# A windowed-attention and mixer kernel: batch 2's q and k turned over by DMA instead of TensorE

## The chip, the cores and the metric

The kernel runs on one core of a Trainium2 chip. The metric is the device time of one execution in microseconds (us): for the kernel before, the median of 3 runs is 300.8 us (300.75, 302.64 and 300.8). One further execution was profiled; the views below are of that one.

## What is computed

Eight batches of attention with 8 heads over 576 positions of 64 elements. Heads 0 to 3 see a plain window of the last 32 positions, heads 4 to 7 a dilated one (every fourth of the last 128). The result, with the heads side by side as 512 channels, goes through a mixer: two matrices over the positions, added back, and two over the channels, added back.

```
q, k, v: [8, 8, 576, 64] float32
scores = (q @ k^T) / 8
plain heads:   0 <= i-j < 32                    dilated heads: 0 <= i-j < 128 and (i-j) % 4 == 0
attn   = softmax over the allowed j;  x = attn @ v   -> [8, 576, 512]
h = relu(x^T @ w_tok1) @ w_tok2;      u = x + h^T      (w_tok1 576x256, w_tok2 256x576)
out = u + relu(u @ w_ch1) @ w_ch2                      (w_ch1 512x1536, w_ch2 1536x512)
```

## The kernel before, in words

**Stages of a batch.** q, k and v are loaded in float32 by DMAs issued on SyncE's queue (SP; `emit_loads_qk`, `load_steps`, `load_v`), cast to float16 by GpSimd (POOL; `cast_steps`, L272), and q and k are turned over so that the 64 elements of two heads lie on the partitions. The four pairs of heads are called hp 0 to 3: hp 0 and 1 are plain, hp 2 and 3 dilated. The turned q stands in `qz[hp]`, one plane for each head with the other head's half zero, k in `kt[hp]`. `scores_plain` (L402) and `scores_dil` (L432) make the scores of one hp in three parts: part 0 and part 1 are the main blocks of the first and the second head, part 2 the rest of both. ScalarE (ACT) takes the exponential into `attp[hp]` or `attd[hp-2]`. From batch 2 on, GpSimd then multiplies the two heads' blocks by the band of allowed pairs (L428, L429 for plain, L454, L455 for dilated); batches 0 and 1 have the band added on TensorE (PE) instead. `values` (L458) makes attention times v for one head, VectorE (DVE) divides by the sums into `xn`, `emit_h1` and `emit_u` are the mixer over positions, `emit_uT` (L530) turns its result over, and `gen_main` (L590) is the mixer over channels: 24 groups `gp` of four matmuls, then the groups `yp`, whose sums DVE adds and SP stores.

**Two ways of turning q and k over.** `transposes` (L291) does it on TensorE: four transposes of 128x128 for q and one for the last 64 positions of q and k, four for k, for each hp; then copies out of PSUM on DVE and ACT. The other way is taken by `by_dma(b)` (L330), before for b >= 3. `dma_steps` (L333) issues five DMA transposes on SP: the tails (`tta`), then q and k of hp 0 and 1 (`qta`, `kra`), then q and k of hp 2 and 3. `place_steps` (L348) copies from there: `plain(hp)` is three copies on GpSimd for hp 0 or 1 (L358 for `kt`, L360 for the two planes of `qz`); `tails`, `dil(0)`, `dil(1)` and `dil_k` are DVE copies (L354, L355, L364, L369). The dilated scores then read k straight from `kra`.

**The order of work.** Nothing is scheduled by a planner at run time. The start (batch 0, L672 to L831) is written out by hand. Then iteration b runs `gen_main(b)`, and `interleave` (L648) puts the stages of the next batches between its groups: each step has a due time in us from the iteration's start, each group and step a cost that is added to a running clock, and a step is emitted once the clock has reached its due time. So the due times give one order of emission, and each engine, and each DMA queue, works through its own share of that order strictly from front to back. A step whose due time comes after the last group of the iteration is emitted at its end, in order of due times.

Iteration 0 holds batch 1's scores, values and mixer over positions, the loads and casts of batch 2, and, before the change, the transposes and scores of batch 2's hp 0 and 1. Iteration 1 holds hp 2 and 3 of batch 2, then its values and mixer, and then the DMA way for batch 3. In the order before, SP meets at the end of iteration 0: the load of v of batch 2 (eight DMAs, L205, due 24.0), the two stores of `yp` s = 2, the two of s = 3, then batch 3's q and k. GpSimd meets the nine casts of q and k of batch 2, the multiplication of hp 0's scores, the eight casts of v, with the multiplication of hp 1 between them.

Of the kernel before, what the change touches and what calls it, by code (L numbers as in the profile page):

```python
# [69 lines left out]
def kernel(  # L70
# [108 lines left out]
    def new_qk(b):  # L179
        for nm in ("q", "k"):  # L180
            for i in range(2):
                l32[(b, nm, i)] = sb.tile([128, 4, 4, D], FP32, tag=f"l_{nm}{i}", bufs=1,
                                          name=f"l_{nm}_{b}_{i}")
        l32[(b, "t")] = sb.tile([128, H, D], FP32, tag="lt", bufs=1, name=f"lt_{b}")

    def load_qk(b, nm, h0, h1, eng):
        i = h0 // 4
        eng.dma_start(
            out=l32[(b, nm, i)][:, h0 - 4 * i:h1 - 4 * i].rearrange("m h r d -> m h (r d)"),
            in_=SRC[nm][b, h0:h1, 0:512, :].rearrange("h (m r) d -> m h (r d)", r=4))  # L190

    def load_tail(b, nm, eng):
        r0 = 64 * (nm == "k")
        eng.dma_start(out=l32[(b, "t")][r0:r0 + 64],
                      in_=SRC[nm][b, :, 512:S, :].rearrange("h s d -> s h d"))
# [20 lines left out]
    def load_v(b):  # L216
        for step in load_v_steps(b):
            step()
# [19 lines left out]
    def emit_loads_qk(b):  # L238
        new_qk(b)
        for nm in ("q", "k"):  # L240
            load_tail(b, nm, nc.sync)
        for h0 in (0, 4):
            for nm in ("q", "k"):
                load_qk(b, nm, h0, h0 + 4, nc.sync)
# [43 lines left out]
    def natural(ap):  # L288
        return ap.rearrange("p (m r) -> p m r", r=4)
# [38 lines left out]
            copy(eng, natural(kt[hp][:, 512:S]), grid[:, :, MR:RS].rearrange("p r m -> p m r"))  # L328

    def by_dma(b):  # L330
        return b >= 3

    def dma_steps(b):  # L333

        def turn_over(t, c):
            nc.sync.dma_start_transpose(out=t, in_=c)

        def half(t, nm, i):
            turn_over(t[:, 2 * i:2 * i + 2].rearrange("p a r m -> p (a r) m"),
                      c16[(b, nm)][:, 2 * i:2 * i + 2].rearrange("m a r h d -> m (a r h d)"))  # L340

        steps = [lambda: turn_over(tta, c16[(b, "t")].rearrange("m h d -> m (h d)"))]
        for i in range(2):
            for t, nm in ((qta, "q"), (kra, "k")):
                steps.append(lambda t=t, nm=nm, i=i: half(t, nm, i))
        return steps

    def place_steps(b):  # L348

        halves = [slice(0, 64), slice(64, 128)]  # L350

        def tails():
            for h in range(2):
                nc.vector.tensor_copy(out=qza[halves[h], :, h, 512:S], in_=tta[halves[h], :, 0:64])  # L354
            nc.vector.tensor_copy(out=kta[:, :, 512:S], in_=tta[:, :, 64:128])  # L355

        def plain(hp):
            nc.gpsimd.tensor_copy(out=natural(kt[hp][:, 0:512]), in_=kra[:, hp].rearrange("p r m -> p m r"))  # L358
            for h in range(2):
                nc.gpsimd.tensor_copy(out=natural(qz[hp][halves[h], h, 0:512]),  # L360
                                      in_=qta[halves[h], hp].rearrange("p r m -> p m r"))

        def dil(h):
            nc.vector.tensor_copy(out=qza[halves[h], 2:4, h, 0:512],  # L364
                                  in_=qta[halves[h], 2:4].rearrange("p a r m -> p a (r m)"))

        def dil_k():
            for hp in (2, 3):
                nc.vector.tensor_copy(out=natural(kt[hp][:, 384:512]),  # L369
                                      in_=kra[:, hp, :, 96:128].rearrange("p r m -> p m r"))  # L370

        return ([lambda hp=hp: plain(hp) for hp in range(2)],
                [tails] + [lambda h=h: dil(h) for h in range(2)] + [dil_k])
# [180 lines left out]
    def score_steps(b, t0, dt, offs=(0.0, 0.7, 2.0), places=None):  # L554

        steps = []
        for hp in range(4):
            at, at_s = places[hp] if places else (t0 + hp * dt, t0 + hp * dt + dt)
            for nm in ("q", "k") if not by_dma(b) else ():
                steps.append((at + 0.9 * (nm == "k"), 0.28, lambda nm=nm, hp=hp: transposes(b, nm, hp)))  # L560
            g = (scores_plain if hp < 2 else scores_dil)(b, hp)
            for i in range(3):
                steps.append((at_s + offs[i], 0.21, lambda g=g: next(g)))
        return steps

    def value_steps(b, t0, dt):
        steps = []
        for h in range(H):
            def step(h=h):
                if h == 0:  # L570
                    xn[b] = sb.tile([128, 5, DM], FP16, tag="xn", bufs=2, name=f"xn_{b}")
                values(b, h)
            steps.append((t0 + dt * h, 0.29 if h < 4 else 0.18, step))
        return steps

    def mix_steps(b, t_h1, t_h1b, t_u, t_uT, du=1.0):
        if b % 2 == 0 and b // 2 not in u16t:
            u16t[b // 2] = sb.tile([128, DM], FP16, tag="u16t", bufs=2, name=f"u16t_{b // 2}")
        h1 = [sb.tile([128, DM], FP16, tag="h1", bufs=4, name=f"h1_{b}_{jb}") for jb in range(2)]
        steps = []  # L580
        for half, at in ((0, t_h1), (1, t_h1b)):
            for jb in range(2):
                steps.append((at + 0.9 * jb, 0.55, lambda jb=jb, half=half: emit_h1(b, jb, half, h1[jb])))
        for i, s in enumerate((4, 0, 1, 2, 3)):
            steps.append((t_u + du * i, 0.44, lambda s=s: emit_u(b, s, h1)))
        for i, cb in enumerate(CBS):
            steps.append((t_uT + 0.9 * i, 0.28, lambda cb=cb: emit_uT(b, cb)))
        return steps
# [136 lines left out]
    va = [st[2] for st in value_steps(0, 0.0, 1.0)]  # L725
# [107 lines left out]
    def at(t0, dt, fs):  # L833
        return [(t0 + dt * i, 0.0, f) for i, f in enumerate(fs)]

    for b in range(B):
        steps = []
        if b == 0:
            steps += score_steps(1, 0, 0, (0.0, 0.6, 1.3),
                                 ((14.0, 16.2), (15.4, 18.2), (17.6, 20.0), (19.0, 21.6)))  # L840
            steps += at(20.0, 0.35, casts1[9:])
            steps += at(20.0, 0.0, [lambda nm=nm: load_qk(2, nm, 4, 8, nc.sync) for nm in ("q", "k")])
            steps += at(24.0, 0.0, [lambda: load_v(2)])
            casts = cast_steps(2)
            va = value_steps(1, 21.7, 0.7)
            steps += va[:4] + [(p + 0.2, c, f) for p, c, f in va[4:]]
            steps += mix_steps(1, 25.6, 28.4, 30.4, 36.2, 1.1)
            steps += score_steps(2, 0, 0, (0.0, 0.7, 1.6),
                                 ((28.8, 31.4), (31.2, 34.6), (0, 0), (0, 0)))[:10]
            steps += at(24.5, 0.5, casts[:9]) + at(34.5, 0.3, casts[9:])  # L850
            steps += at(36.0, 0.0, [lambda: emit_loads_qk(3)])
        elif b == 1:
            late = score_steps(2, -4.3, 2.4, (0.0, 0.7, 1.6))
            va = value_steps(2, 4.2, 1.0)
            steps += late[10:] + va[:4] + [(9.6 + (0.0, 0.8, 2.8, 3.6)[i], c, f) for i, (_, c, f) in enumerate(va[4:])]
            steps += mix_steps(2, 10.8, 14.6, 17.2, 22.2)
            steps += score_steps(3, 22.2, 2.8) + at(9.0, 0.6, cast_steps(3))
            steps += at(6.0, 0.0, [lambda: load_v(3)]) + at(20.0, 0.9, load_steps(4))
            steps += at(15.0, 0.7, dma_steps(3)) + at(20.6, 0.4, place_steps(3)[0])
            steps += [(t, 0.0, f) for t, f in zip((21.6, 27.0, 27.8, 28.6), place_steps(3)[1])]  # L860
        else:
            if b + 1 < B:
                steps += value_steps(b + 1, 0.6, 1.1) + mix_steps(b + 1, 6.6, 10.6, 13.2, 18.2)
            if b + 2 < B:
                steps += at(2.0, 0.6, cast_steps(b + 2)) + score_steps(b + 2, 18.6, 2.7)
                steps += at(8.5, 0.7, dma_steps(b + 2)) + at(14.8, 0.4, place_steps(b + 2)[0])
                steps += [(t, 0.0, f) for t, f in zip((17.3, 21.8, 22.6, 23.4), place_steps(b + 2)[1])]
            if b + 3 < B:
                steps += at(13.0, 0.9, load_steps(b + 3))
        interleave(gen_main(b), steps)  # L870
# [30 lines left out]
```

## Time and profile before

| what | value |
|---|---|
| median of 3 runs | 300.8 us |
| the profiled execution, its own time | 300.74 us |
| its span from first to last instruction | 298.7 us |
| granted TensorE clock, mean | 0.997 |
| busy: PE, DVE, ACT, POOL | 286.8, 159.3, 140.8, 180.1 us |
| iteration 0, from the first `gp` to the next iteration's first | 29.8 to 69.8 us |
| iteration 1 | 69.8 to 107.1 us |

How to read the views: PE is TensorE's matmul, PEld its weight load, which overlaps. A row of the timeline gives the start in us from the span's beginning, the time that the group took, the engine, the line of the kernel, the operation, output and input with their shapes, and how many instructions are merged. What stands in brackets is the idle time of the engine before the group and what ended it. The time of a matmul is its whole passage; back to back, the next one starts earlier, so the cost of a group on a busy PE is the distance from its start to the next group's start. SPq rows are DMA issues on SyncE's queue: their time is that of the issue, and the landing stands in a column of its own on the page.

### The profile page before, as it was taken

What the parts mean: (1) busy time and instruction counts of PE and PEld (TensorE: products, weight loads), DVE (VectorE), ACT (ScalarE), POOL (GpSimd) and SP (SyncE); (2) the same over time, 40 slices, a digit from 0 to 9 for tenths busy, and PEclk for the clock granted to TensorE, in tenths of its full rate; (3) what the DMA queues carried; (4) which work ended last, traced back from release to release, by engine and by line L of the source; (5) the groups of instructions that cost most, each with busy time, mean ns of one, the idle gap of its engine ahead of it and who ended that gap; (6) DMA issues with size and microseconds to landing.
All of it is one profiled execution on the core that took longest, in us unless ns stands there. A gap on an engine that the chain in (4) does not pass through costs nothing.

```text
span 298.7 us, 7805 instructions
## 1 busy us (share of the span) xinstructions
PE 286.8 (96%) x3112; PEld 257.2 (86%) x3112; DVE 159.3 (53%) x357; ACT 140.8 (47%) x319; POOL 180.1 (60%) x244
## 2 busy tenths in 40 slices
PE   5789999998999999999999999999999999999995
PEld 2687999987987999899987999899988999899794
DVE  5875438756737965643645254644745264532122
ACT  2853436377652545455545536365554535304500
POOL 7882056429998899739992999449992930000000
PEclk9999999999999999999999999999999999999998
DMA  7999999966997999984599749964551220022023
GB/s 219 270 212 177 214 312 222 326 165 188 286 196 128 279 288 154 280 211 151 69 205 276 211 111 153 307 139 146 120 55 35 72 72 0 3 71 72 2 70 105
DMA packets 91443, 49.10 MB, mean 164 GB/s; under 512 B 59760, under 2 KB 90352, under 8 KB 91408
## 3 DMA queue, kind: packets, MB, share of 16 engines
q1 hardware_dynamic: 87168, 43.53, 59.7%
q0 software_dynamic: 2640, 3.91, 7.4%
q10 hardware_dynamic: 1600, 1.18, 1.3%
q8 instruction: 24, 0.39, 0.6%
q14 instruction: 11, 0.09, 0.1%
HBM read 37.04 MB, written 9.44 MB: 156 GB/s over the span
## 4 chain that ended last, share of the span: by engine, by line
PE 92%; DVE 3%; DMA 2%; ACT 1%; issue 1%; ACTq 0%; POOLq 0%
PE gp L602 31%; PE yp L619 28%; PE sc L393 4%; PE h1p L499 4%; PE up L511 4%; PE yp L639 3%; DMA const<-consts 2%; PE sm L393 1%; PE tpu L548 1%; PE av L469 1%; PE h1p L497 1%; PE av L480 1%; PE tpu L540 1%; PE up L524 1%; PE av L467 1%; PE sc L391 1%
## 5 line engine op out<-in xcount | busy, mean ns | idle before, releaser
L602 PE MATMUL gp<-uT,w 128*128 128x288 f16 x768 | 109.9, 286 | 0.7 <-ACT uT L101 0.6
L619 PE MATMUL yp<-w,gt 128*128 128x256 f16 x756 | 95.6, 273 | 0.0
L107 ACT ACTIVATE gt<-gp 128x288 f16<-128x288 f32 x138 | 56.6, 410 | 72.1 <-PE gp L602 65.9
L602 PEld LDWEIGHTS <-w 128*128 128x128 f16 x768 | 83.1, 113 | 8.2 <-issue 1.2
L619 PEld LDWEIGHTS <-gt 128*128 128x128 f16 x768 | 75.9, 106 | 3.7
L113 POOL TENSOR_TENSOR attp<-attp,const 128x1280 f16<-128x1280 f16 (+1 forms) x24 | 36.0, 1529 | 32.9 <-ACT attp L422 32.9
L629 DVE TENSOR_TENSOR o<-yp,u 128x512 f32<-128x512 f32 x31 | 21.3, 689 | 50.6 <-PE yp L619 44.2
L109 DVE TENSOR_SCALAR gt<-gp 128x288 f16<-128x288 f32 x54 | 24.6, 455 | 35.5 <-PE gp L602 33.5
L113 POOL TENSOR_TENSOR attd<-attd,const 128x1024 f16<-128x1024 f16 (+1 forms) x24 | 32.8, 1397 | 0.0
L113 DVE TENSOR_TENSOR xn<-av,rec 128x320 f16<-128x320 f32 x64 | 31.5, 491 | 2.2
L393 PEld LDWEIGHTS <-kt 128*128 128x128 f16 x272 | 22.5, 101 | 3.1 <-DVE kt L302 1.6
L103 POOL CAST c_q<-l_q 128x512 f16<-128x512 f32 x31 | 18.9, 613 | 6.4 <-DMA l_q<-in_q_dram 5.7
L413 ACT ACTIVATE attp<-sc 128x480 f16<-128x480 f32 x32 | 18.0, 572 | 9.5 <-PE sc L393 9.4
L518 DVE TENSOR_TENSOR u<-up,xn 128x512 f16<-128x512 f32 x26 | 17.9, 691 | 8.0 <-PE up L511 8.0
L360 POOL COPY qz<-qt 64x512 f16<-64x512 f16 x20 | 21.4, 1072 | 0.6
L442 ACT ACTIVATE attd<-sc 128x512 f16<-128x512 f32 x32 | 18.9, 597 | 5.3 <-PE sc L393 4.7
L488 DVE RECIPROCAL rec<-av 128x5 f32<-128x5 f32 x64 | 12.2, 191 | 14.3 <-PE av L475 7.2
L393 PE MATMUL sc<-qz,kt 128*128 128x160 f16 (+1 forms) x144 | 18.6, 228 | 1.3 <-DVE kt L302 1.3
L103 POOL CAST c_k<-l_k 128x512 f16<-128x512 f32 x29 | 18.0, 622 | 3.0 <-DMA l_k<-in_k_dram 1.3
L101 ACT COPY uT<-tpu 128x576 f16<-128x576 f16 x15 | 9.6, 640 | 16.3 <-PE tpu L549 16.3
L107 ACT ACTIVATE h<-h1p 128x256 f16<-128x256 f32 x28 | 10.7, 383 | 10.1 <-PE h1p L499 8.0
L639 PE MATMUL yp<-w,gt 128*128 128x512 f16 x48 | 12.0, 379 | 0.0
(131 smaller groups left out, 444.4 us busy)
## 6 DMA issues: line engine op xcount, KB each, us to landing
out_dram<-o SPq DMA_DIRECT2D x72, 128.0 KB, 2.5
l_q<-in_q_dram SPq DMA_DIRECT2D x15, 512.0 KB, 6.4
l_k<-in_k_dram SPq DMA_DIRECT2D x14, 512.0 KB, 7.4
l_vn<-in_v_dram SPq DMA_DIRECT2D x32, 128.0 KB, 6.7
l_vd<-in_v_dram SPq DMA_DIRECT2D x16, 256.0 KB, 3.9
w<-in_moe_w_ch_dram POOLq DMA_DIRECT2D x6, 512.0 KB, 7.6
lt<-in_q_dram SPq DMA_DIRECT2D x8, 128.0 KB, 4.4
l_vt<-in_v_dram SPq DMA_DIRECT2D x8, 128.0 KB, 4.3
```

Source lines behind the costliest of these rows:

```text
L103: eng.tensor_copy(out=out, in_=in_)
L107: nc.scalar.activation(out=out, in_=in_, func=AF.Relu)
L109: eng.tensor_scalar_max(out=out, in0=in_, scalar1=0.0)
L113: eng.tensor_tensor(out=out, in0=x, in1=y, op=ALU.mult)
L360: nc.gpsimd.tensor_copy(out=natural(qz[hp][halves[h], h, 0:512]), in_=qta[halves[h], hp].rearrange("p r m -> p m r"))
L393: nc.tensor.matmul(out=out, lhsT=lhsT, rhs=qz[hp][:, h, queries], start=hide is None, stop=True)
L413: nc.scalar.activation(out=blocks[:, h, 0:3, 0:BLK], in_=p[:, 0:3 * BLK].rearrange("p (b c) -> p b c", c=BLK), func=AF.Exp, scale=0.125)
L442: nc.scalar.activation(out=a[:, h, 0:DTL], in_=p, func=AF.Exp, scale=0.125)
L602: nc.tensor.matmul(out=p[:, 0:288], lhsT=w3[cb][:, 512 * (mb // 4) + mb % 4:512 * (mb // 4) + 512:4], rhs=uT[(b, cb)][:, 288 * sh:288 * sh ...
L619: nc.tensor.matmul(out=p[:, c], lhsT=gt[(b // 2, mb)][:, a0:m0 + 512:4] if half else gt[(b // 2, mb)][:, a0:a0 + 128], rhs=w4[mb][:, c], s ...
L629: nc.vector.tensor_tensor(out=o32, in0=p, in1=u16[(b, s)], op=ALU.add)
L639: nc.tensor.matmul(out=p, lhsT=gt[(b // 2, mb)][:, 512:640], rhs=w4[mb], start=(mb == 0), stop=(mb == NMB - 1))
```

## The change

`by_dma` holds from b = 2 on, so batch 2's transposes on TensorE and their copies are gone and its dilated scores read `kra`. In iteration 0, instead of the transposes and the scores of hp 0 and 1, there are the five DMA transposes of batch 2 on SP, the six plain copies on GpSimd and, as the last step, the three tail copies on DVE. In iteration 1 all four hp's scores are due from 0.3 on, `dil(0)`, `dil(1)` and `dil_k` on DVE from 1.0 on, and the values and the mixer of batch 2 have later due times.

```
     def by_dma(b):
-        return b >= 3
+        return b >= 2
...
             steps += mix_steps(1, 25.6, 28.4, 30.4, 36.2, 1.1)
-            steps += score_steps(2, 0, 0, (0.0, 0.7, 1.6),
-                                 ((28.8, 31.4), (31.2, 34.6), (0, 0), (0, 0)))[:10]
             steps += at(24.5, 0.5, casts[:9]) + at(34.5, 0.3, casts[9:])
+            steps += [(t, 0.0, f) for t, f in zip((27.0, 30.0, 30.7, 33.0, 33.7), dma_steps(2))]
+            steps += at(34.4, 0.0, place_steps(2)[0]) + at(39.0, 0.0, place_steps(2)[1][:1])
             steps += at(36.0, 0.0, [lambda: emit_loads_qk(3)])
         elif b == 1:
-            late = score_steps(2, -4.3, 2.4, (0.0, 0.7, 1.6))
-            va = value_steps(2, 4.2, 1.0)
-            steps += late[10:] + va[:4] + [(9.6 + (0.0, 0.8, 2.8, 3.6)[i], c, f) for i, (_, c, f) in enumerate(va[4:])]
-            steps += mix_steps(2, 10.8, 14.6, 17.2, 22.2)
+            steps += score_steps(2, 0, 0, (0.0, 0.7, 1.6), ((0, 0.3), (0, 2.3), (0, 4.3), (0, 6.3)))
+            steps += at(1.0, 0.9, place_steps(2)[1][1:])
+            va = value_steps(2, 0.0, 1.0)
+            steps += [((6.8, 7.6, 9.0, 9.8, 12.0, 12.8, 14.8, 15.6)[i], c, f) for i, (_, c, f) in enumerate(va)]
+            steps += mix_steps(2, 11.6, 17.0, 19.4, 24.6)
```

Worked through `interleave`, the order after the change is as follows. SP: load of v of batch 2, stores of s = 2, transposes of the tails and of q of hp 0 and 1, stores of s = 3, transposes of k of hp 0 and 1, of q and of k of hp 2 and 3, batch 3's q and k. GpSimd: casts of q and k of batch 2, `plain(0)`, `plain(1)`, the eight casts of v, then the multiplications of hp 0, 1, 2, 3, then batch 3's casts. TensorE in iteration 1: one `gp` group, part 0 of hp 0, one group, part 1, two groups, part 2, part 0 of hp 1, one group, part 1, one group, part 2, and so on; the values of head 0 come behind ten groups, those of head 2 behind thirteen, of head 4 behind seventeen, of head 6 behind twenty.

## The prediction, as put on record before the change was run

> **What bounds the kernel now.** I read the page first, then busy time by stretch, then the timeline of each engine's queue around the edit.
>
> ```profile
> PE 286.8 (96%) x3112; PEld 257.2 (86%) x3112; DVE 159.3 (53%) x357; ACT 140.8 (47%) x319; POOL 180.1 (60%) x244
> ```
> ```profile
> 29.80:69.80 40.00, 38.73 (x468) 35.80 (x467) 23.91 (x53) 20.61 (x47) 17.46 (x30) 1.00 0.92 239
> 69.80:107.10 37.30, 36.94 (x412) 32.96 (x409) 25.98 (x49) 20.17 (x47) 35.18 (x43) 1.00 0.96 228
> ```
>
> The columns of the second fence are the stretch, its length, the busy time of PE, PEld, DVE, ACT and POOL, the granted clock, the DMA share and GB/s. The first row is iteration 0, the second iteration 1. TensorE is the bound in both: 38.73 of 40.00 and 36.94 of 37.30 us. Work taken off it comes back as time, and a wait put onto it is paid in full, for there is hardly any idle time later that would take it up. The second thing to see is GpSimd: half idle in iteration 0, but 35.18 of 37.30 us in iteration 1. The change adds GpSimd work just at this border.
>
> **What is taken off TensorE.** The turning of one q and its tail:
>
> ```profile
> 60.75 0.39 PE L297 MATMUL tp_q<-const,c_q 128*128 128x128 f16 x4
> 60.97 0.22 PE L317 MATMUL tp_q<-const,c_t 128*128 128x128 f16 x1
> 61.03 0.27 PE L497 MATMUL h1p<-xn,w1t 128*128 128x256 f16 x1
> ...
> 70.57 0.90 PE L602 MATMUL gp<-uT,w 128*128 128x288 f16 x6 [0.36 <-ACT uT L101]
> ```
>
> From start to start a q costs 0.28 us (60.75 to 61.03), a k 0.22 (60.75 to 60.97, the same four transposes). That is 0.50 for each hp, **2.0 us** for four. Their copies on DVE and ACT go too, but those engines are two thirds busy at most, so I count nothing for them. The scores are only moved: six parts of hp 0 and 1, about 0.2 us each, leave iteration 0. So iteration 1's first group, which ends about 70.8 (0.24 behind the last start above), would end at 70.8 - 1.0 - 1.2 = 68.6. The next instruction on TensorE is part 0 of hp 0, and it needs what GpSimd has placed. With the scores gone, the short waits in the chain of batch 1's mixer (0.36 above) may grow by some tenths; that only shifts 68.6, and the wait that follows ends with GpSimd and not with TensorE.
>
> **When the placing can start.** SP's queue and the issues of the DMA transposes of batch 3, which show what those of batch 2 will cost:
>
> ```profile
> 54.84 4.21 SPq L205 DMA_DIRECT2D l_vn<-in_v_dram  x4
> ...
> 62.06 0.93 SPq L635 DMA_DIRECT2D out_dram<-o  x2
> ```
> ```profile
> 83.77 1.23 SPq L336 DMA_TRANSPOSE qt<-c_q  x1
> 85.10 1.28 SPq L336 DMA_TRANSPOSE kr<-c_k  x1
> ```
> ```profile
> out_dram<-o SPq DMA_DIRECT2D x72, 128.0 KB, 2.5
> ...
> kr<-c_k SPq DMA_TRANSPOSE x10, 3.8
> ```
> ```profile
> DMA to landing us min/median/max: 3.2/3.8/5.0
> ```
>
> SP is held by the load of v of batch 2 from 54.84 on and reaches the two stores of s = 2 at 62.06, done at 62.99. Up to there its order is the same in both kernels. Only now come the transposes, about 1.35 us apart (83.77 to 85.10) where two stores take 0.93 together: tails at 63.05, q at 64.4, then the two stores of s = 3 (0.93 us; their sums are made by then, since the work ahead of them on TensorE is shorter), and **k of hp 0 and 1 at about 66.7**. The casts are no limit:
>
> ```profile
> 61.72 0.61 POOL L103 CAST c_k<-l_k 128x512 f16<-128x512 f32 x1
> 66.73 2.99 POOL L113 TENSOR_TENSOR attp<-attp,const 128x1280 f16<-128x1280 f16 x2 [4.40 <-ACT attp L422]
> 69.67 1.42 POOL L103 CAST vv<-l_vn 128x256 f16<-128x256 f32 x4
> ...
> 72.17 2.99 POOL L113 TENSOR_TENSOR attp<-attp,const 128x1280 f16<-128x1280 f16 x2
> 75.12 0.61 POOL L103 CAST vv<-l_vd 128x512 f16<-128x512 f32 x1
> 75.68 0.39 POOL L103 CAST vt<-l_vx 128x256 f16<-128x256 f32 x1
> 76.04 5.48 POOL L113 TENSOR_TENSOR attd<-attd,const 128x1024 f16<-128x1024 f16 x4
> 81.47 0.60 POOL L103 CAST c_t<-lt 128x512 f16<-128x512 f32 x1
> ...
> 86.49 1.43 POOL L103 CAST vv<-l_vn 128x256 f16<-128x256 f32 x4
> ...
> 89.90 1.06 POOL L358 COPY kt<-kr 128x512 f16<-128x512 f16 x1
> 90.91 2.19 POOL L360 COPY qz<-qt 64x512 f16<-64x512 f16 x2
> ```
>
> The last cast ends at 62.33, four us before that issue. A transpose of k lands 3.2 to 5.0 us behind its issue, so 69.9 to 71.7; I take the median, **70.5**. GpSimd stands idle from 62.33 until then, and everything it still has to do is queued behind `plain(0)`.
>
> [...] The rows differ: 3.8 us to landing against 2.5 for a store of 128 KB. With a store's landing the whole result below would be 1.3 us lower, 307.1.
>
> **What the lateness costs.** An hp is placed in 3.25 us (1.06 and 2.19): `kt`, then 1.1 for each plane of `qz`. So hp 0's first head is ready at 72.6, its second at 73.75; hp 1's at 75.85 and 77.0. TensorE goes from row to row in these steps: a `gp` group 0.49, a plain part 0.21.
>
> ```profile
> 82.50 0.65 PE L602 MATMUL gp<-uT,w 128*128 128x288 f16 x4
> 82.99 0.28 PE L480 MATMUL av<-vv,attd 128*128 128x65 f16 x4
> ...
> 95.56 0.37 PE L393 MATMUL sc<-qz,kt 128*128 128x160 f16 x3
> 95.77 0.82 PE L619 MATMUL yp<-w,gt 128*128 128x256 f16 x6
> ```
>
> Front wait: at part 0, 72.6 - 68.6 = 4.0. Then 0.21 and 0.49 lead to 73.3, and part 1 waits 0.45 for 73.75. Two groups and two parts (1.4) lead to 75.15; part 0 of hp 1 waits 0.7 for 75.85. At 76.55 its part 1 waits 0.45 for 77.0. Together **5.6 us**.
>
> Second wait: the casts of v now stand behind the placing and ahead of every multiplication. They cost 2.5 (69.67 to 72.17) and 0.92 (75.12 to 76.04), so 3.42, to 80.4. The multiplication of a plain hp takes 2.94 (66.73 to 69.67), so hp 0 is done at 83.35, hp 1 at 86.3, and with 2.72 for a dilated one (76.04 to 81.47 holds two) hp 2 at 89.0, hp 3 at 91.75. TensorE, from part 1 of hp 1 at 77.0, has five groups and six parts ahead of head 0's values (3.6 us) and is there at 80.6: it waits **2.75 us**. Head 2 is 2.35 us further on by the same steps, at 85.7, and waits 0.6. Head 4 comes at 89.35 and head 6 at 91.7, both about when their hp is done.
>
> Third, batch 3: its nine casts (81.47 to 86.49, 5.0 us) run from 91.75, its casts of v until 100.2, `plain(0)` of batch 3 has hp 0's heads ready at 102.3 and 103.45. TensorE reaches hp 0 about 10.4 us behind head 6, at 102.15, and waits 0.15 and 0.55, so **0.7**. GpSimd ends batch 3's multiplications near 118 with iteration 2 starting near 115, and their readers wait for nothing.
>
> Other edits at nothing: the DVE copies of batch 2 run while GpSimd copies, and there a copy is prolonged to about a microsecond (two of the tails took 1.24, below). What is queued behind them are `relu`s of `gp` whose banks are needed three groups later; without that cover each would cost up to the 2.7 us that one of two copies took here:
>
> ```profile
> 93.08 1.24 DVE L354 COPY qz<-tt 64x256 f16<-64x256 f16 x2
> ```
> ```profile
> 98.10 3.17 DVE L364 COPY qz<-qt 64x1024 f16<-64x1024 f16 x2
> ```
>
> Batch 3's q and k are issued after the transposes, about 3 us later than now; GpSimd casts them at 91.75 in place of 81.47, so this is covered. The tail's landing and `tails` on DVE come before 70 and are covered by the wait for k.
>
> The sum: 5.6 + 2.75 + 0.6 + 0.7 = 9.65 us of waits, less 2.0 of work, is +7.65. As a check, 107.1, where iteration 2 begins (the end of the second stretch above), becomes 91.75 + 22.3 (the costs of the steps that are left in the iteration) + 0.7 = 114.75. Behind that TensorE has no idle time to give. The profiled execution's own time is 300.74 (span 298.7 and 2.04 around it), 0.06 below the median shown: **308.4 us**.
>
> **The rivals.** *The placing is in time (faster).* Then only the 2.0 us are left and the time is 298.7. For it speaks that GpSimd idles 4.40 us just there. Against it: the copies would have to start by 68.6 - 2.1 = 66.5, and k's transpose is not even issued then. It decides if SP gets through the load of v some 4 us sooner, or if TensorE reaches part 0 that much later. Chance 0.10. *Loss and gain are equal*: k lands so early that the front wait is about 2 and the values find their scores ready; 300.7, chance 0.06. *Only the front wait*: head 0's values come late enough for the multiplication; 300.74 + 5.6 - 2.0 = 304.3. The rows put 12.85 us of GpSimd work between the landing and head 0, TensorE 10.1, so I give it 0.14. *A cold TensorE*: at the start, before it has worked, its matmuls are slow, and four idle us could bring that back. The price:
>
> ```profile
> 2.54 3.59 PE L667 MATMUL idle_p<-idle 128*128 128x512 f16 x8 [2.54 <-POOL idle L156]
> ```
> ```profile
> 89.24 1.03 PE L639 MATMUL yp<-w,gt 128*128 128x512 f16 x4
> ```
>
> Eight matmuls of 512 take 3.59 us there; four take 1.03 later, so 0.22 for each one more and 1.9 for eight. The loss is 1.7 us. Part of it would fall into the second wait, which GpSimd ends. In full it gives 310.1; chance 0.10, since no row of before shows an idle stretch of that length in mid-kernel. [...]
>
> **How the numbers follow.** The forecast, 308.4, has 0.60. Its own range follows from the landing of k, which shifts the whole chain: 3.2 us after the issue gives 307.8, 5.0 gives 309.6, and with the cold clock on top 311.3. Downwards the range reaches to the front wait alone with an early landing, 304.3 - 0.6 = 303.7. I set 303.5 to 311.0, which leaves out the first two rivals, 0.16. Of the first rival, 0.7% below now, I count 0.04 as faster by over 1% and 0.06 as within 1% (about what a measurement of this kernel can tell from no change); with the second rival that is 0.12 within 1%, and slower by over 1% are the other three, 0.84.
>
> **What would show it.** Right: GpSimd idle from about 62.3 to 70 ahead of L358; k's transpose issued after 66; TensorE waiting about 4 us for GpSimd's `qz` ahead of the first plain scores and 2 to 3 us for `attp` ahead of head 0; iteration 2 starting near 114.75. Wrong: L358 starting before 67, TensorE without a wait above 1 us at either place, or transposes issued ahead of the load of v.

## The result, and the profile after

The changed kernel takes **313.8 us** (median of 4 runs, 313.29 to 315.35) where the kernel before takes 301.36 in the same job (4 runs, 300.75 to 302.64): a ratio of **1.042**, interval 1.036 to 1.047. It is slower, as forecast, but by 12.4 us in place of 7.7, and the time lies 2.8 us above the upper end of the range. The profiled execution took 314.09 us, its span is 311.6.

The page first: the engines' busy time and the granted clock by slices.

```profile
PE 291.5 (94%) x3076; PEld 258.6 (83%) x3076; DVE 160.6 (52%) x354; ACT 138.0 (44%) x313; POOL 187.0 (60%) x250
...
PEclk9999999997999899999999999999999999999999
```

TensorE has 36 matmuls fewer, yet is busy 4.7 us longer. The clock row shows one reason: it dips in two slices of 7.8 us, the 10th (from 70.1) and the 14th (from 101.3). In the kernel before, neither of these does.

One thing has to be set aside before the two timelines are compared. In this execution the first 16 us took 1.66 us longer than in the profiled one of before: its first matmuls keep the slow pace of the start until after 10 us (a matmul on line 391 takes 0.34 us there, and 0.23 from 7.29 on before). The same row of iteration 0 starts at 30.23 instead of 28.57:

```profile
30.23 1.05 PE L602 MATMUL gp<-uT,w 128*128 128x288 f16 x5 [0.20 <-ACT uT L101]
```

In the profiles of the experiments below that row starts anywhere from 28.2 to 30.5, whatever was edited, so it is no effect of the change. (In the profile of before, the first `gp` of iteration 0 stands at 27.96, just ahead of this row, and not at 29.8 as in the table ahead of the prediction.) Times below are as the profile has them; "less 1.66" puts them on the scale of the prediction, and this row serves as the common one between profiles.

**The front.** SyncE's queue, then GpSimd's, at the border of iterations 0 and 1:

```profile
63.95 1.34 SPq L336 DMA_TRANSPOSE tt<-c_t  x1
65.39 1.25 SPq L336 DMA_TRANSPOSE qt<-c_q  x1
66.73 1.02 SPq L635 DMA_DIRECT2D out_dram<-o  x2
67.84 1.24 SPq L336 DMA_TRANSPOSE kr<-c_k  x1
```
```profile
61.49 0.62 POOL L103 CAST c_k<-l_k 128x512 f16<-128x512 f32 x1
71.18 1.04 POOL L358 COPY kt<-kr 128x512 f16<-128x512 f16 x1 [9.07 <-DMA kr<-c_k]
...
81.56 5.55 POOL L113 TENSOR_TENSOR attp<-attp,const 128x1280 f16<-128x1280 f16 x3
```

The order in SP's queue is the forecast one: tails, q, stores of s = 3, k. GpSimd idles 9.07 us for k (8.2 forecast, 62.33 to 70.5) and the first multiplication starts at 81.56, less 1.66 at 79.9 (80.4 forecast).

**What TensorE waits for.** All its bracketed waits between 72 and 107 us of above 0.3, with the rows where head 6's values and iteration 2 begin:

```profile
73.24 0.56 PE L393 MATMUL sc<-qz,kt 128*128 128x160 f16 x3 [2.90 <-POOL qz L360]
...
84.21 0.20 PE L469 MATMUL av<-vv,attp 128*128 128x65 f16 x1 [2.03 <-POOL attp L113]
...
92.77 0.28 PE L480 MATMUL av<-vv,attd 128*128 128x65 f16 x4
...
106.38 0.23 PE L548 MATMUL tpu<-const,u 128*128 128x128 f16 x1 [3.05 <-DVE u L518]
106.97 0.23 PE L548 MATMUL tpu<-const,u 128*128 128x128 f16 x1 [0.37 <-DVE u L518]
...
120.45 1.14 PE L602 MATMUL gp<-uT,w 128*128 128x288 f16 x8
```

The first two waits are the forecast ones, at the forecast places. The third is not: it stands ahead of the turning of batch 2's mixer result (`emit_uT`), not at batch 3's scores, and DVE ends it. Iteration 2 begins at 120.45, less 1.66 at 118.8, where 114.75 was forecast. Head 6's values came at 92.77, less 1.66 at 91.1 (91.7 forecast): up to there the chain held within a microsecond, and everything that is missing was lost between head 6 and iteration 2.

DVE's queue just there:

```profile
100.59 0.68 DVE L518 TENSOR_TENSOR u<-up,xn 128x512 f16<-128x512 f32 x1
101.18 3.44 DVE L354 COPY qz<-tt 64x256 f16<-64x256 f16 x2
104.63 1.08 DVE L355 COPY kt<-tt 128x256 f16<-128x256 f16 x1
105.64 1.27 DVE L518 TENSOR_TENSOR u<-up,xn 128x512 f16<-128x512 f32 x2
```
```profile
101.36 1.06 POOL L358 COPY kt<-kr 128x512 f16<-128x512 f16 x1
102.37 2.17 POOL L360 COPY qz<-qt 64x512 f16<-64x512 f16 x2
104.60 1.04 POOL L358 COPY kt<-kr 128x512 f16<-128x512 f16 x1
```
```profile
L354 DVE COPY qz<-tt x12: 207/224/2337, 69.9 to 238.1; 64x256 f16<-64x256 f16 x12
```

The last two of the four sums that `emit_uT` needs stand behind batch 3's three tail copies, and these take 4.5 us together. The third fence (least, median and most ns of one copy on line 354) shows that such a copy takes 0.22 us at the median; here one took 2.34. Held against the fence of GpSimd's rows, the DVE copies end where GpSimd copies end: 104.62 against 104.54, 105.71 against 105.64.

How did the tails come to stand there? The diff doesn't touch them: they are due at 21.6 as before. But it moves batch 2's mixer from 17.2 to 19.4, so that of its four sums two now come after 21.6; before, all four came ahead of it.

The clock of the stretches (the length, then busy time of PE, PEld, DVE, ACT, POOL, the granted clock, DMA share and GB/s):

```profile
72.00:74.00 2.00, 0.76 (x5) 0.74 (x6) 0.00 (x0) 0.10 (x1) 1.94 (x3) 0.76 0.82 163
74.00:76.00 2.00, 2.00 (x12) 1.37 (x10) 1.17 (x3) 1.04 (x2) 1.94 (x3) 0.50 0.82 131
76.00:78.00 2.00, 1.81 (x18) 1.35 (x17) 1.97 (x3) 1.54 (x5) 1.88 (x3) 0.89 1.07 372
...
106.00:108.00 2.00, 1.26 (x12) 1.13 (x13) 0.92 (x2) 0.71 (x2) 1.69 (x2) 0.79 0.91 307
108.00:110.00 2.00, 2.00 (x15) 1.63 (x13) 0.59 (x2) 0.98 (x2) 0.00 (x0) 0.50 1.03 335
110.00:112.00 2.00, 2.00 (x25) 1.91 (x23) 1.12 (x3) 1.18 (x4) 0.48 (x1) 0.85 1.10 354
```

Behind the first and the third wait TensorE gets half its clock for 3.4 us: a mean of 0.76 over 2 us is 0.96 us at half, 0.89 is 0.44, and with the 2.0 between them that makes 3.4; the second place gives the same (0.84, 2.0 and 0.6). So the slow stretches run from 73.04 to 76.45 and from 107.17 to 110.58. Behind the second wait, 2.03 us, there is none.

### The profile page after: what moved, and what is told of

The parts are those of the page before. It is cut to its first block, busy times and chain, and to the rows that moved or that the text cites. A ratio compares the mean times of both kernels' runs of the same rounds, so it can differ in the third digit from the quotient of the medians.

```text
span 311.6 us, 7741 instructions
## 1 busy us (share of the span) xinstructions
PE 291.5 (94%) x3076; PEld 258.6 (83%) x3076; DVE 160.6 (52%) x354; ACT 138.0 (44%) x313; POOL 187.0 (60%) x250
## 4 chain that ended last, share of the span: by engine, by line
PE 85%; DVE 5%; DMA 3%; ACT 2%; POOL 2%; issue 1%; SPq 0%; POOLq 0%; ACTq 0%
PE gp L602 29%; PE yp L619 26%; PE sc L393 4%; PE h1p L499 4%; PE up L511 3%; PE yp L639 3%; POOL attp L113 2%; DMA const<-consts 2%; PE sm L393 1%; PE tpu L548 1%; PE av L469 1%; PE h1p L497 1%; PE av L480 1%; DVE qz L354 1%; PE tpu L540 1%
## 5 line engine op out<-in xcount | busy, mean ns | idle before, releaser
L602 PE MATMUL gp<-uT,w 128*128 128x288 f16 x768 | 111.1, 288 | 0.5 <-DVE uT L103 0.2
L360 POOL COPY qz<-qt 64x512 f16<-64x512 f16 x24 | 25.9, 1081 | 0.7
L358 POOL COPY kt<-kr 128x512 f16<-128x512 f16 x12 | 12.8, 1070 | 9.6 <-DMA kr<-c_k 9.1
```

What stands on the lines that cost most here:

```text
L602: nc.tensor.matmul(out=p[:, 0:288], lhsT=w3[cb][:, 512 * (mb // 4) + mb % 4:512 * (mb // 4) + 512:4], rhs=uT[(b, cb)][:, 288 * sh:288 * sh ...
```

## The experiments

Theory A, made from these rows: the 4 to 5 us that the forecast lacks come from the tail copies of batch 3, which stand ahead of the last two `u` sums and are held while GpSimd works. Its rival: these copies simply wait for their data, since their transpose is issued late too. Further theories concern the front, the clock, and whether a better order of the same work would gain. The times of before in these jobs were 300.8 to 301.2.

### The third wait: e1, e2 and e7

e1 moves the tails behind all four sums:

```
-            steps += [(t, 0.0, f) for t, f in zip((21.6, 27.0, 27.8, 28.6), place_steps(3)[1])]
+            steps += [(t, 0.0, f) for t, f in zip((24.5, 27.0, 27.8, 28.6), place_steps(3)[1])]
```

> Batch 3's three tail copies on DVE are due 24.5 in place of 21.6, so they stand behind the last two sums of batch 2's mixer and not ahead of them. Theory A (the 3.05 us wait of TensorE for DVE's sum near 106, and the half clock behind it, come from those copies being held while GpSimd copies): both go, the time falls by about 4.5 us, from 313.8 to about 309.3. Rival (TensorE would wait at batch 3's plain scores anyway, because GpSimd is late): it falls by 1 us at most, to about 312.8.

Measured: 309.23 us (308.72 to 309.96), ratio 1.026, interval 1.021 to 1.031. Of the timeline of e1:

```profile
103.23 0.69 DVE L518 TENSOR_TENSOR u<-up,xn 128x512 f16<-128x512 f32 x1 [0.40 <-PE up L511]
103.84 1.43 DVE L354 COPY qz<-tt 64x256 f16<-64x256 f16 x2
```
```profile
103.68 0.52 PE L548 MATMUL tpu<-const,u 128*128 128x128 f16 x4
...
105.24 0.37 PE L393 MATMUL sc<-qz,kt 128*128 128x160 f16 x3 [0.48 <-POOL qz L360]
```

The last sum ends before the copies begin, `emit_uT` waits for nothing, and the time falls by 4.6 us. In the traces, the stretch from head 6's values to iteration 2 takes 23.38 us in e1 (93.41 to 116.79) and 27.68 after the change (92.77 to 120.45). These 4.3 us are 3.4 of waits, less two new waits of 0.48 and 0.17 at batch 3's plain scores, and about 1.5 for the slow stretch, which is gone too. The two new waits (0.65) stand where the forecast had its third wait, 0.7.

e2 leaves the order and gives these three copies to ScalarE:

```
+            eng = nc.scalar if b == 3 else nc.vector
...
-                nc.vector.tensor_copy(out=qza[halves[h], :, h, 512:S], in_=tta[halves[h], :, 0:64])
-            nc.vector.tensor_copy(out=kta[:, :, 512:S], in_=tta[:, :, 64:128])
+                copy(eng, qza[halves[h], :, h, 512:S], tta[halves[h], :, 0:64])
+            copy(eng, kta[:, :, 512:S], tta[:, :, 64:128])
```

> Batch 3's three tail copies on ScalarE in place of DVE, the order unchanged. Theory A (a DVE copy from SBUF to SBUF is held by a GpSimd instruction that runs beside it, and a ScalarE copy is not): the copies take well under 1 us each although GpSimd copies at that time, and the time is near 309.3, as with the copies late. Rival (the copies are late because their data are): on ScalarE they end as late as on DVE, about 105.7 in the profile's time.

Measured: 309.27 us (308.72 to 310.17), ratio 1.026, interval 1.021 to 1.031, the same as e1. ScalarE's rows in e2:

```profile
97.22 0.82 ACT L101 COPY qz<-tt 64x256 f16<-64x256 f16 x2
98.06 0.40 ACT L101 COPY kt<-tt 128x256 f16<-128x256 f16 x1
```

0.4 us for each copy. The common row of iteration 0 starts at 28.69 in e2, 1.54 ahead of the one above; so these 97.22 are 98.8 on that scale, 2.4 us before DVE began the copies. The data were there. The rival fell; the copies were held on DVE.

A row of e2 also bears on the front, where its kernel is that of the change:

```profile
72.82 0.56 PE L394 MATMUL sc<-qz,kt 128*128 128x160 f16 x3 [4.04 <-POOL qz L361]
```

Here the front wait is 4.04 us and not 2.90, k having come 1.1 us later on the common scale. So the front differs between executions by about a microsecond with nothing edited.

e7 takes the kernel before and moves its tails ahead of the last two sums, and changes nothing else:

```
-            steps += [(t, 0.0, f) for t, f in zip((21.6, 27.0, 27.8, 28.6), place_steps(3)[1])]
+            steps += [(t, 0.0, f) for t, f in zip((19.3, 27.0, 27.8, 28.6), place_steps(3)[1])]
```

> The kernel before with one due time changed: batch 3's three tail copies on DVE at 19.3 in place of 21.6, so that they stand ahead of the last two sums of batch 2's mixer, as in the changed kernel, while GpSimd copies beside them. Theory A: the sums come 2 to 3 us later, TensorE waits for them ahead of uT, the time rises by 2 to 3.5 us, to 303 to 304.5. Rival (the order of these copies matters only with the rest of the change): no change, 300.8.

Measured: 304.37 us (302.54 to 304.5), ratio 1.009, interval 1.006 to 1.013; the profiled execution is the fastest of the four. Its rows:

```profile
90.99 1.83 DVE L354 COPY qz<-tt 64x256 f16<-64x256 f16 x2
92.85 1.07 DVE L355 COPY kt<-tt 128x256 f16<-128x256 f16 x1
```
```profile
94.58 0.23 PE L548 MATMUL tpu<-const,u 128*128 128x128 f16 x1 [1.52 <-DVE u L518]
```

So the order alone, in a kernel without the change, costs 3.45 us at the median and 1.5 + 0.4 us of waits in the execution that the trace shows. With e1 and e2 the third wait is shown from both sides.

### The front: e4, e3 and e6

e4 puts batch 2's casts of v into GpSimd's idle time ahead of the placing:

```
-            steps += at(24.5, 0.5, casts[:9]) + at(34.5, 0.3, casts[9:])
+            steps += at(24.5, 0.5, casts[:9]) + at(30.0, 0.3, casts[9:])
```

> GpSimd's eight casts of v of batch 2 stand ahead of the placing, in the time in which it waits for k's transpose. Theory B (the wait ahead of head 0's values is the 3.4 us of v casts between the placing and the first multiplication): the front wait stays, the waits of 2.0 and 0.3 us ahead of heads 0 and 2 go, 311.5. Rival (v lands so late that the casts push the placing back): the front wait grows and the time is 313.8 or more.

Measured: 309.39 us (309.35 to 309.93), ratio 1.026, interval 1.021 to 1.032: 4.4 us gained where 2.3 were expected. Of the timeline of e4, GpSimd and then TensorE:

```profile
70.51 1.04 POOL L358 COPY kt<-kr 128x512 f16<-128x512 f16 x1 [3.72 <-DMA kr<-c_k]
```
```profile
72.59 0.56 PE L393 MATMUL sc<-qz,kt 128*128 128x160 f16 x3 [3.96 <-POOL qz L360]
...
102.20 0.23 PE L548 MATMUL tpu<-const,u 128*128 128x128 f16 x1 [2.60 <-DVE u L518]
```

The placing still waits for k, the front wait is 3.96, and the wait for head 0's `attp` is gone, with the casts out of its way. That shows the second wait's cause. Why the gain is larger than that wait can be read from the traces in part: from the common row to iteration 2 it is 87.68 us in e4 (28.54 to 116.22), 2.54 less than after the change, and a further 1.69 by which the two profiled executions differ lie in the start, which no edit here touches. How the executions without a profile divide isn't known.

e3 issues batch 2's first three transposes, the one of k among them, ahead of the load of v:

```
-            steps += at(24.0, 0.0, [lambda: load_v(2)])
+            steps += at(28.6, 0.0, [lambda: load_v(2)])
...
-            steps += [(t, 0.0, f) for t, f in zip((27.0, 30.0, 30.7, 33.0, 33.7), dma_steps(2))]
+            steps += [(t, 0.0, f) for t, f in zip((25.1, 26.6, 28.5, 33.0, 33.7), dma_steps(2))]
```

> The load of v of batch 2 stands behind the transposes of the tails, q and k of hp 0 and 1 in SP's queue, and the two stores of s = 3 and the last two transposes behind that load. Theory B (the front wait and its half clock come from k's transpose standing behind the load of v): k is issued near 61.5, GpSimd's placing starts near 65 and the front wait of 2.9 us and the half clock behind it go; v lands later, so the wait ahead of head 0's values stays at about 2 us. About 4.5 us less, 309.3. Rival (the transposes are late for a reason of their own, such as the DMA engines being full): placing starts no earlier than 70, no gain.

Measured: 314.45 us (313.27 to 315.31), ratio 1.043, interval 1.037 to 1.048: no gain at all, a miss. The front did what it should, GpSimd starts placing at 67.09 and no plain score waits longer than 0.66 us. The time was lost 10 us later. DVE, GpSimd and TensorE in e3:

```profile
77.78 8.09 DVE L369 COPY kt<-kr 128x128 f16<-128x128 f16 x2 [1.08 <-DMA kr<-c_k]
```
```profile
77.57 5.92 POOL L113 TENSOR_TENSOR attp<-attp,const 128x1280 f16<-128x1280 f16 x4
83.46 2.11 POOL L113 TENSOR_TENSOR attd<-attd,const 128x1024 f16<-128x1024 f16 x1
```
```profile
77.80 0.40 PE L393 MATMUL sc<-qz,kr 128*128 128x128 f16 x4 [2.64 <-DMA kr<-c_k]
...
86.29 1.12 PE L602 MATMUL gp<-uT,w 128*128 128x288 f16 x4 [7.37 <-DVE gt L109]
```
```profile
L369 DVE COPY kt<-kr x12: 253/271/7914, 77.8 to 243.8; 128x128 f16<-128x128 f16 x12
```

This is the clearest picture of the hold. A DVE copy that takes 0.27 us at the median, the first of the two, took 7.91: it lasted through five multiplications that GpSimd ran back to back, and ended at 85.69, just after GpSimd went idle at 85.57. Behind it in DVE's queue stood one `relu` of `gp`, and TensorE waited 7.37 us for it.

The hold goes beyond one instruction of GpSimd: the first four of the five took 5.92 us together and the fifth 2.11, and the copy ended only behind the fifth. ScalarE's copies of the tails took 0.4 us each in e2.

e6 is e3 with the copies of `tails`, `dil` and `dil_k` of batches 2 and 3 on ScalarE, and batch 2's dilated ones later (the same edit at L364 and L369):

```
+            pe = nc.scalar if b <= 3 else nc.vector
...
-                nc.vector.tensor_copy(out=qza[halves[h], :, h, 512:S], in_=tta[halves[h], :, 0:64])
+                copy(pe, qza[halves[h], :, h, 512:S], tta[halves[h], :, 0:64])
...
-            steps += at(1.0, 0.9, place_steps(2)[1][1:])
+            steps += at(4.25, 0.0, place_steps(2)[1][1:])
```

> As the run with the load of v behind k's transpose, and with the tail copies and the dilated copies of batches 2 and 3 on ScalarE in place of DVE (those of batch 2 due 4.25). Theory A and B together (the front wait comes from k behind the load of v; the 7.4 us wait for DVE in that run, and the wait ahead of the last uT, come from DVE copies held by GpSimd): both go, what is left is about 2.6 us for the last transposes of q and k and 1 to 2 us ahead of the values: 303 to 304. Rival (the late load of v and the late last transposes move the loss and do not end it): 308 or more.

Measured: 305.31 us (304.44 to 306.18), ratio 1.014, interval 1.011 to 1.017. Off DVE, the copies cost neither the 7.4 us nor the third wait: 9.1 us less than e3, though 1.3 us more than the upper end of what was expected. What is left in e6:

```profile
75.35 0.38 PE L393 MATMUL sc<-qz,kr 128*128 128x128 f16 x4 [2.03 <-ACT qz L101]
```
```profile
78.00:80.00 2.00, 1.59 (x13) 1.19 (x12) 0.00 (x0) 1.58 (x4) 2.00 (x2) 0.50 1.05 356
```

ScalarE's own copies are late now, since the last transposes of q and k, behind the load of v, land only at 74.26. In this execution half the clock is granted once more, from 77.0 to 83.8; in the other three, 304.44 to 305.64 us, it stayed at 1.00.

### The clock: e5 and e10

Both fill the front wait with matmuls on idle data ahead of the first plain scores, to keep the clock up, 12 in e5 and 24 in e10 (shown); nothing else is edited.

```
+            steps += at(0.29, 0.0, [lambda: warm(24)])
```

> Twelve matmuls of 512 columns on zeros (0.216 us each, 2.6 in all) stand on TensorE ahead of the first plain scores of batch 2, in the time in which it waits for GpSimd. They compute nothing that is used. Theory C (the stretch of granted clock 0.50 behind the front wait is a loss of its own): the clock stays at 1.00 there, the work that took 3.6 us takes about 2.1 plus what it waits for GpSimd, about 0.3 to 1.0 us less, 313.0. Rival (the half clock only fills a wait for GpSimd that would be there anyway): same time, 313.8.

> Twenty-four idle matmuls (5.2 us) in place of twelve ahead of batch 2's first plain scores, so that TensorE has work through nearly all of the front wait. They compute nothing that is used. Theory C (the half clock follows on the stretch without work): granted clock 1.00 behind the front wait, hp 0's and hp 1's scores limited by the placing alone, about 0.5 us less at head 0's values, which GpSimd ends; 313.3. Rival (the clock falls for another reason, such as zeros or the load of the first 70 us): it still shows 0.5.

Measured: e5 314.15 us (312.27 to 315.0), ratio 1.042, interval 1.038 to 1.046; 12 were too few, TensorE still idled 2.98 us, so e5 tells nothing. e10: four executions of 308.36, 312.81, 314.63 and 314.94 us, too far apart for one number. The profiled one is that of 308.36, with the clock at 1.00 throughout. In it:

```profile
82.71 0.20 PE L469 MATMUL av<-vv,attp 128*128 128x65 f16 x1 [1.73 <-POOL attp L113]
...
102.74 0.23 PE L548 MATMUL tpu<-const,u 128*128 128x128 f16 x1 [0.93 <-DVE u L518]
```

Head 0's values start at 82.71; after the change it was 84.21, less 1.66, 82.55. Warm or cold, the front ends at the same time, since GpSimd sets it: the slow clock there is hidden by the second wait. This execution is 5.7 us shorter than the profiled one of the changed kernel. Of that, 1.7 lie in the start and 3.8 between head 6 and iteration 2 (23.90 us, 91.27 to 115.17, in place of 27.68). The third wait there is 0.93 + 0.37 in place of 3.05 + 0.37, 2.1 less, because the three tail copies took 2.4 us and not 4.5 in the same order of both queues. No slow stretch follows it, and the remaining 1.7 us are about its price, near the 1.5 of e1. So how long the copies are held differs by microseconds where the order is the same; whether it is this that spreads the four executions isn't shown, as only one has a trace.

### Together, and as a better order: e11, e8, e9 and e12

e11 is e4 and e1 in one.

> The changed kernel with two of the single edits together: GpSimd's casts of v ahead of the placing, and batch 3's tail copies due 24.5. If the wait ahead of the values and the wait ahead of uT are losses of their own, the two gains (4.4 and 4.5 us) add up: 313.8 - 8.9 = 304.9. Rival (they are one backlog seen twice): 307 to 309.

Measured: 306.14 us (305.68 to 306.66), ratio 1.016, interval 1.011 to 1.021. It gains 7.7 us on the changed kernel, where e1's 4.6 and e4's 4.4 make 9.0: in the main two losses side by side, not one backlog seen twice. The traces say the same: from head 6 to iteration 2 it takes 23.36 us, as e1 did (23.38).

e8 removes all three waits that are known. The casts of v come first, k is transposed ahead of the stores of s = 3, batch 2's plain placing is taken from GpSimd, all copies of batch 3 stand behind the mixer's sums, and scores, values and mixer are due later. The core of it:

```
+                copy(nc.vector if b == 2 else nc.gpsimd, natural(kt[hp][:, 0:512]),
+                     kra[:, hp].rearrange("p r m -> p m r"))
...
+                copy(nc.scalar if b == 2 else nc.gpsimd, natural(qz[hp][halves[h], h, 0:512]),
+                     qta[halves[h], hp].rearrange("p r m -> p m r"))
...
+            steps += [(t, 0.0, f) for t, f in zip((27.0, 28.6, 29.0, 33.0, 33.7), dma_steps(2))]
+            steps += score_steps(2, 0, 0, (0.0, 0.7, 1.6), ((0, 3.3), (0, 4.6), (0, 6.3), (0, 8.3)))
+            steps += at(0.6, 0.0, place_steps(2)[0][:2]) + at(1.5, 0.0, place_steps(2)[0][2:])
```

> A version built on the findings: GpSimd's casts of v ahead, k's transpose ahead of the stores of s = 3, batch 2's plain placing on ScalarE (qz) and DVE (kt) and not on GpSimd, the plain scores of batch 2 due 3 us later, its values, mixer and batch 3's scores 2.5 to 3 us later, batch 3's tail copies behind the mixer's sums. If the waits are what the theories say, TensorE has gp groups to work on until k has landed and no wait above 1 us is left: the 2.0 us of transposes come back, 298.8 to 300. Rival (something else in the change costs time, such as DMA load or GpSimd's extra work in the next iteration): above 301.5.

Measured: 303.4 us (302.75 to 305.12), ratio 1.008, interval 1.005 to 1.011. That is a miss, above the 301.5 from which the rival began. One long wait is left, which the new order itself makes. ScalarE and TensorE in e8:

```profile
70.14 4.35 ACT L101 COPY qz<-qt 64x512 f16<-64x512 f16 x4
```
```profile
74.97 1.14 PE L608 MATMUL gp<-uT,w 128*128 128x288 f16 x8 [3.22 <-ACT gt L107]
```

Four copies in a row stand ahead of the `relu`s. e9 sets them apart, two on ScalarE one at a time and two on DVE, which GpSimd, now idle there (busy for 0.00 us between 68 and 74), doesn't hold (0.6 us each):

```
+                copy((nc.scalar if h == hp else nc.vector) if b == 2 else nc.gpsimd,
+                     natural(qz[hp][halves[h], h, 0:512]), qta[halves[h], hp].rearrange("p r m -> p m r"))
...
+            steps += score_steps(2, 0, 0, (0.0, 0.7, 1.6), ((0, 3.0), (0, 4.3), (0, 6.3), (0, 8.3)))
+            steps += [(t, 0.0, f) for t, f in zip((0.6, 0.6, 1.5, 2.2, 1.5, 2.2), place_steps(2)[0])]
```

> As the reworked version, with the four ScalarE copies of qz, which stood in one row ahead of the relus there and cost TensorE 3.2 us, taken apart: two on ScalarE, one at a time, and two on DVE, and the plain scores 0.3 us earlier. If that wait was the only one of weight, it falls by about 3 us, from 303.4 to 300.3 or a little less, so to the kernel before or up to 1 us below it. Rival (the change has another cost that shows in no wait): 302 or more.

Measured over 12 runs: **300.6 us** (300.06 to 302.34) against 300.86 for the kernel before, ratio 0.999, interval 0.996 to 1.001: the same. The forecast 2.0 us less of TensorE work doesn't come out as time even in an order without a wait above 0.51 us. Taking the distance from each TensorE row's start to the next, less the bracketed idle, from 28.57 to iteration 2 (107.13 before, 107.10 in e9), the transposes' rows shrink by 2.28 us, a little over the forecast; the bracketed idle grows by 0.60, and the remaining rows by 1.65, in amounts under 0.5 that the view doesn't bracket. The densest of them in e9:

```profile
73.26 0.65 PE L608 MATMUL gp<-uT,w 128*128 128x288 f16 x4
73.90 0.36 PE L399 MATMUL sm<-qz,kt 128*128 128x160 f16 x4
74.37 0.37 PE L399 MATMUL sc<-qz,kt 128*128 128x160 f16 x3
```

The group lasts 0.64 to the next start, not 0.49, and the part behind it 0.47, not 0.2. Three such places between 73 and 76 make 0.5 us; the rest of the 1.65 is spread more thinly. e12 sets the score parts of e9 further apart to get these back:

```
-            steps += score_steps(2, 0, 0, (0.0, 0.7, 1.6), ((0, 3.0), (0, 4.3), (0, 6.3), (0, 8.3)))
+            steps += score_steps(2, 0, 0, (0.0, 1.0, 2.0), ((0, 3.0), (0, 5.3), (0, 7.8), (0, 10.3)))
```

> e9_rework2 with the plain and dilated score parts of batch 2 set further apart in iteration 1 (hp starts 3.0, 5.3, 7.8, 10.3 in place of 3.0, 4.3, 6.3, 8.3; parts 1.0 apart in place of 0.7 and 0.9). The whole reference is computed. In e9_rework2 the transposes that are gone save 2.3 us of TensorE between the first group of iteration 0 and that of iteration 2, yet iteration 2 starts no earlier. Theory: about 1.1 us of it is given back where the parts follow one another so closely (71.5 to 79.5) that each waits a tenth or a quarter of a us for the buffer of the one before; set apart they cost the bare 0.2 us each: 299.5 to 300.0. Rival: the time is given back elsewhere (the mixer ahead of the iteration, the end of the iteration): 300.3 to 300.9, as e9_rework2. A second rival: the later scores make GpSimd's multiplications late for the values: above 301.

Measured: 302.06 us (301.82 to 303.93, 12 runs) against 301.23, ratio 1.003, interval 1.002 to 1.005. The second rival, and it shows in e12's trace:

```profile
91.05 0.29 PE L486 MATMUL av<-vv,attd 128*128 128x65 f16 x4 [1.13 <-POOL attd L113]
91.68 0.20 PE L489 MATMUL av<-vt,attd 128*128 128x65 f16 x1 [0.33 <-POOL attd L113]
```

The plain parts run at their bare cost now, but GpSimd's last multiplications come too late for the values, 1.8 us with one more wait of 0.34. Between scores that crowd and multiplications that are late there is little room: from GpSimd's first multiplication to iteration 2 (75.0 to 107.1 in e9) GpSimd is busy for 31.8 of 32.1 us, TensorE for 31.6. Whether another order gains a part of the 2 us stays open; none tried here did.

## Why the forecast went wrong, point by point

**What bounds the kernel** held: TensorE, with no slack later in the iteration. The waits that e1, e2 and e4 removed came back as time. That work taken off TensorE comes back as time too, which the prediction says in the same place, did not show in e9.

**Work taken off TensorE**: 2.0 us forecast, 2.28 by the rows of e9. Right as work; as time it came out in none of the orders tried, since the one that avoids the waits, e9, gives it back. What it is worth in the changed kernel isn't shown.

**When the placing can start** held: the queue's order, GpSimd idle for k, k landing 3.3 us after its issue (67.84 to 71.18) where 3.8 was taken. Less 1.66, k came at 69.5 instead of 70.5. The issue at 67.84, less 1.66, is 66.2 (66.7 forecast). The landing of a store, 2.5 us, with which the prediction came to 307.1, would have fitted no better: 2.5 us behind the issue is 70.3 in this profile, 3.8 is 71.6, and the measured 71.18 lies between.

**The front wait** was 2.90 + 0.19 in place of 5.6, and cost about as much: part 1 of hp 1 started at 77.92, less 1.66 at 76.3, forecast 77.0. The short waits of 0.45, 0.7 and 0.45 that the forecast put between the parts were filled with the same work at half the clock.

**The second wait** was 2.03 + 0.28 in place of 2.75 + 0.6, its cause shown by e4; on the common scale head 0 came at 82.55 (83.35 forecast), so the sum of both places was forecast 0.8 us too high for this execution. That is no more than executions differ by: in e2, with the same kernel up to there, k came at 70.6 on that scale (70.5 forecast), the front wait was 4.04 (4.0 forecast at that place) and head 0 came at 83.7.

**The step that failed** is the one that set the other edits at nothing, and with it the third term. "What is queued behind them are `relu`s of `gp`" was looked at for batch 2's copies alone. For those it was right in the changed kernel, and wrong by 7.4 us in e3. Batch 3's tail copies were not moved by the diff, so I did not look at them; but the mixer's later due times moved two `u` sums behind them. The third wait was sized 0.7, at batch 3's scores, and measured 3.05 + 0.37, ahead of `emit_uT` and ended by DVE. The row of the prediction that shows a DVE copy of two taking up to 2.7 us had the price in it; what lacked was the queue order on DVE around batch 3.

**The cold TensorE**, a rival of 0.10 priced at 1.7 us, happened, behind the first and the third wait. At the front it was covered, as the rival's own sentence allowed (e10 and the changed kernel reach head 0 at 82.7 and 82.55). Behind the third wait it isn't covered, and it cost about 1.5 by e1 and 1.7 by e10. The range stopped at 311.0, short even of the prediction's own 311.3 for a late k and a cold clock.

The prediction had no idle stretch of that length in mid-kernel to go by and put this as a chance, priced from the eight matmuls of the start. The runs show the half clock, but the length of one wait doesn't decide it: it followed 2.90 us of idle after the change and 2.03 in e6, with one more wait of 0.19 between, while the 2.03 of the second wait after the change and 3.22 in e8 left the clock at 1.00. The slow stretches begin at 73.04 and 107.17 after the change, 34.13 us apart, ten times the 3.41 that each of them lasts; in e6 the half clock lasts 6.8 us and in e3 10.2, about two and three times as much. If the trace of the changed kernel is divided into stretches of 3.41 us, from 73.04 on and back, the two ahead of the slow ones have 2.91 and 2.99 us without a matmul, and no other between 20 and 308 us has more than 1.39. In e6 the 3.41 us ahead of 77.0 have about 1.95 (73.6 to 75.35, and 0.19). So the idle part of such a stretch fits these two traces better than the length of one wait. That is my estimate from them; how e8's 3.22 us lie in such stretches isn't shown.

**The account.** From the common row of iteration 0 to iteration 2 it is 107.13 - 28.57 = 78.56 us before and 120.45 - 30.23 = 90.22 after, 11.7 more. The forecast's 7.65, less 0.6 up to head 6 (91.1 in place of 91.7), plus 2.7 for the third wait (3.42 in place of 0.7), plus 1.5 for the slow stretch behind it, plus 0.4 for the steps from head 6 on (22.73 in e1 without its two waits, 22.3 in the prediction) are 11.7. The medians differ by 12.4. The remaining 0.7 is within what executions of the same code differ by, as the start and the front of e2 show, and isn't settled closer.

## What to carry to other kernels

When a change moves due times, print the new order of every engine's queue and look at each pair that swapped, also among steps that the diff doesn't name: the largest single loss in the changed kernel came from three copies that kept their due time while their neighbours moved. A VectorE copy from SBUF to SBUF beside busy GpSimd showed no fixed price here (0.27 us alone, up to 7.9), so what stands behind it decides where it may go: behind the sums that TensorE waits for, on ScalarE (0.4 us a copy in e2), or where GpSimd is idle. And work taken off the bounding engine is time only if the way round it meets its deadlines on the other engines; here the best order tried came out even.

## What the runs showed of the hardware that I had not expected

- A DVE copy of 0.27 us was held 7.9 us, through five GpSimd instructions back to back (e3). With its neighbour it took 8.09 us there, and the two took 0.74 on ScalarE in e6, beside a GpSimd that was busy for 2.00 of 2.00 us.
- The length of this hold differs where the order is the same: 4.5 us for the three tail copies after the change, 2.4 in e10.
- The granted clock fell to 0.50 for 3.41 us at two places after the change, for 6.8 us in e6 and for 10.2 in e3. The length of one wait did not decide it: it followed waits of 2.03 and 0.19 us in e6, and did not follow one of 3.22 in e8.
